# A list scheduler's numbers replaced in a one-core sparse attention and SwiGLU kernel

## The chip, the cores and the metric

The kernel runs on one core of a Trainium2 chip. The metric is the device time of one launch in microseconds, as the median of several runs. The chip has five engines that each follow their own instruction list in order: PE (matrix products), DVE (vector work), ACT (activation functions and copies), POOL (the third element-wise engine, here also the gathers) and SP (which here only starts transfers). They wait for one another through semaphores.

## The reference, cut to what matters

```python
# q, k, v: [4 batches, 8 heads, 768 rows, 64]; sampled_blocks: [24, 3]
scores = matmul(q, k.T) / sqrt(64)
mask = |row//32 - col//32| <= 1                     # window of 3 blocks
mask |= row block 0 or 23, or column block 0 or 23  # full rows and columns
mask |= column block in sampled_blocks[row block]   # 3 random blocks
attn = exp(scores - max) / (sum + 1e-9)             # over the masked entries
x = matmul(attn, v).transpose(0, 2, 1, 3).reshape(3072, 512)
g, val = x @ w_gate, x @ w_val                      # 512 -> 1536
out = (g * sigmoid(g) * val) @ w_out                # 1536 -> 512
```

All inputs are single precision values that reach the kernel as 64-bit words. The three weights are 512 x 1536, 512 x 1536 and 1536 x 512.

## The kernel before

The 3072 tokens are worked in eight chunks of 384 (half a batch each, three tiles of 128 tokens). A chunk is attention over its 12 query blocks of 32 rows with all 8 heads (11 sparse blocks and one full row block), and then the feed-forward part (FFN) on the 384 tokens. Names such as `b2.1.4` are chunk 2, tile 1, block 4.

Ahead of everything stand the inputs. Weights come in 36 pieces of 512 KB (L389) into a ring of four buffers (`w1raw`, `w2raw`), and three DVE operations turn each piece into single precision (`to_f32`, L382 to L384: one "decode"). Each piece is squared and summed on ACT (L361, `wsq`) and later split into a high and a low half-precision part (ACT L354, DVE L357). K and V of a batch come in three transfers each (L511), are squared and summed on ACT (L361), normalised to a power of two (PE L351, DVE L533 and L342 to L346) and split (L354, L357). K of batch 0 is then turned by PE (L583) and copied to `kst` by ACT and DVE (L593, L591); V goes back to memory (`vd`, L617) and is read again block by block (L1011 to L1013 on SP, and a gather on POOL, L1016) into `vring`. Queries come at L684 and L744, are split, and are spread out by L755 into `qs` (four transfers each).

One sparse block of attention is a chain: copy of its random K blocks into `kring` (L1002 to L1005; on POOL for chunk 0, else on DVE), scores on PE (L1051 and L1060 in chunks 0 and 1, L1030 after), maximum on DVE (L1069 or L1076), exponential on ACT (L1095), reciprocal on DVE, split of the probabilities (ACT L354, DVE L357), a transposing transfer that SP starts (L1155, `pts<-pp`), and the product with V on PE (L1168, `pv`). In chunk 0 PE transposes the probabilities instead (L1115, with copies at L1124 and L1128). The full row blocks run through L806, L817 to L835, L858 and L875. The FFN of chunk 0 works in single precision (`ffn_first`, L1255 and L1291), so that it needs decoded weights and not split ones; the FFN of the others uses half precision parts (`ffn`: first layer L1369 with 12 products for each of the 24 half-pieces, tanh L1373, products on DVE L1376 and L1379, split L1387 on ACT and L1390 on POOL, second layer L1416, out through L1305 and L1315).

The order is not written out by hand. Each piece of work is a task, given by `add(engine, microseconds, emit, needs, rank, ...)`. `Plan.order` runs a simulated clock over all tasks: an engine that is free takes, among the tasks whose needs have ended and whose buffers are free, the one of lowest rank. The rank is a base number plus an entry of the table `SHIFT` (L41 to L89) for the task's name. The order in which tasks are taken is the order in which their instructions are emitted, so that it fixes each engine's program; the numbers of microseconds are used for nothing else. `in_turn` keeps the blocks of one stage in the same order. A transfer is a task on SP with a duration `dma` of its own, which runs on one simulated queue and ends `DMA_US` later. The four lines that do this are

```python
t.rank = rank + SHIFT.get(t.key, 0.0)
if best is not None and (t.rank, t.no) > (best.rank, best.no): continue
queue = max(queue, t.end) + t.dma
t.end = queue + DMA_US
```

Of the kernel before, what the change touches and what calls it, by code (L numbers as in the profile page):

```python
# [11 lines left out]
I32 = mybir.dt.int32  # L12
# [8 lines left out]
DM, DF, DO = H * D, 1536, 512  # L21
# [11 lines left out]
K0, V0, TAB = -6.0, -3.0, -2.0  # L33
EVAC = -100.0
V_AT = 0.0
DMA_US = 2.0
SEM_US = 0.1
# [1473 lines left out]
```

## Time and profile before

| what | value |
|---|---|
| median of 3 runs | 847.31 us (847.08 to 849.96) |
| the profiled execution, its own time | 845.61 us |
| span of the profiled execution | 843.8 us |
| mean granted PE clock | 0.965 |
| PE busy | 769.2 us, 91% of the span |
| DVE, ACT, POOL busy | 592.1 us (70%), 528.4 us (63%), 200.7 us |
| bytes moved | 144.05 MB |

The profile is one execution. "Busy" is the time in which an engine executes; the wait of an instruction is the idle time just ahead of it, put down to what ended it. The granted clock is the share of PE's full speed that it had. The rest between the span and the run's own time (1.8 us) lies outside the recorded instructions.

### The profile page before, as it was taken

The page shows a single profiled execution, that of the slowest core. Times are in us where ns is not written, and L with a number is a line of the kernel's source. Part 1 is how long each engine was busy: PE and PEld are TensorE (multiplying, and loading weights), DVE is VectorE, ACT ScalarE, POOL GpSimd, SP SyncE. Part 2 cuts the span into 40 slices and gives each one's busy share as a digit, 9 for nine tenths or more (in the row PEclk, how much of TensorE's full clock was granted, in tenths as well). Part 3 has the DMA queues.
Part 4 walks back from the last instruction along what each step waited for, and adds up shares of the span by engine and source line. Part 5 has one row for each costly group of instructions (what it writes and reads, how often), then busy time and mean ns, then how long its engine had stood idle before and what let it go on. Part 6 is the DMA issues. An engine that isn't in the chain of part 4 may idle for free.

```text
span 843.8 us, 20625 instructions
## 1 busy us (share of the span) xinstructions
PE 769.2 (91%) x7634; PEld 460.9 (55%) x7634; DVE 592.1 (70%) x1784; ACT 528.4 (63%) x1266; POOL 200.7 (24%) x258
## 2 busy tenths in 40 slices
PE   0267799979999999999999999998999999999997
PEld 0246655545465655665566556663566556655653
DVE  5987989858888976896488757852679769821320
ACT  5855845669786766788467757873458658821220
POOL 5574100002014321231223211321123212310220
PEclk9757999989999999999999999999999999999999
DMA  9999785789947897899878876988847964820001
GB/s 292 256 280 274 213 241 164 146 200 185 220 128 220 186 228 138 191 180 232 218 179 180 182 167 132 199 173 243 210 96 143 193 145 103 169 57 26 1 1 38
DMA packets 196309, 144.05 MB, mean 171 GB/s; under 512 B 133104, under 2 KB 156272, under 8 KB 196208
## 3 DMA queue, kind: packets, MB, share of 16 engines
q1 hardware_dynamic: 190576, 125.42, 65.2%
q0 software_dynamic: 5632, 17.31, 8.3%
q8 instruction: 60, 0.98, 0.5%
q14 instruction: 41, 0.34, 0.1%
HBM read 86.58 MB, written 12.58 MB: 118 GB/s over the span
## 4 chain that ended last, share of the span: by engine, by line
PE 68%; DMA 15%; DVE 7%; ACT 3%; issue 3%; SPq 2%; POOL 1%; DVEq 0%; ACTq 0%; POOLq 0%
PE p L1369 33%; PE po L1416 13%; DMA pts<-pp 6%; PE pv L1168 6%; PE p L1255 5%; PE po L1291 4%; PE qk L1030 3%; DMA w<-vd 2%; DVE w L383 2%; DVE w L384 1%; PE pvf L875 1%; DMA qn<-in_q_dram 1%; DMA kraw<-in_k_dram 1%; PE qkf L806 1%; DMA qs<-qraw 1%
## 5 line engine op out<-in xcount | busy, mean ns | idle before, releaser
L1369 PE MATMUL p<-xt,w 128*128 128x384 f16 x2016 | 340.3, 326 | 0.0
L1369 PEld LDWEIGHTS <-w 128*128 128x128 f16 x2016 | 191.9, 98 | 128.4 <-issue 6.2
L1416 PE MATMUL po<-w,h 128*128 128x512 f16 x756 | 171.1, 381 | 0.0
L1390 POOL TENSOR_TENSOR h<-act,h 128x384 f16<-128x384 f32 x84 | 80.0, 953 | 304.4 <-ACT h L1387 304.1
L1016 POOL DMA_INDIRECT vring<-vd,vidx x82 | 78.6, 959 | 280.4 <-PE pv L1168 236.9
L1416 PEld LDWEIGHTS <-h 128*128 128x128 f16 x756 | 71.9, 98 | 87.2 <-issue 7.1
L1376 DVE SCALAR_TENSOR_TENSOR act<-act,p 128x384 f32<-128x384 f32 x84 | 46.1, 549 | 64.3 <-ACT act L1373 62.6
L1168 PEld LDWEIGHTS <-vring 128*128 128x128 f16 x1968 | 68.9, 99 | 28.2 <-issue 16.2
L357 DVE SCALAR_TENSOR_TENSOR pp<-e,rr,pp 128x256 f16<-128x256 f32 x152 | 77.7, 552 | 7.5 <-ACT pp L354 6.2
L1168 PE MATMUL pv<-pts,vring 128*128 128x64 f16 x1968 | 72.3, 194 | 11.0 <-DMA pts<-pp 6.3
L1373 ACT ACTIVATE act<-p,gsc 128x384 f32<-128x384 f32 x84 | 48.4, 577 | 52.8 <-PE p L1369 45.2
L1095 ACT ACTIVATE e<-e,nb,es 128x256 f32<-128x256 f32 x132 | 78.2, 593 | 2.2
L1387 ACT CAST h<-act 128x384 f16<-128x384 f32 x84 | 42.5, 505 | 54.4 <-DVE act L1379 53.9
L354 ACT ACTIVATE pp<-e,rr 128x256 f16<-128x256 f32 x152 | 67.8, 497 | 10.3 <-DMA ptsf<-ppf 3.6
L1255 PE MATMUL p<-xt,w 128*128 128x384 f32 x192 | 70.1, 520 | 1.3 <-ACT xt L1134 1.0
L1379 DVE SCALAR_TENSOR_TENSOR act<-act,hs,p 128x384 f32<-128x384 f32 x84 | 51.3, 611 | 22.9 <-PE p L1369 21.7
L1255 PEld LDWEIGHTS p<-xt,w 128*128 128x128 f32 x192 | 37.6, 202 | 27.6 <-issue 5.3
L1076 DVE CUSTOM_DVE_ANT_1 e<-qk,msk 128x256 f32<-128x256 f32 x132 | 50.0, 416 | 0.5 <-PE qk L1030 0.3
L1005 DVE COPY kring<-kst 128x256 f16 x228 | 46.0, 258 | 4.9 <-PE pv L1168 1.6
L1305 ACT ACTIVATE ot<-po,oc 128x512 f32<-128x512 f32 x21 | 14.4, 686 | 52.7 <-PE po L1416 52.2
L1194 DVE TENSOR_TENSOR xt<-pv,xt 64x256 f16<-64x256 f32 x76 | 31.9, 420 | 17.2 <-ACT xt L1189 14.1
L361 ACT ACTIVATE wsq<-w 128x512 bf16<-128x512 f32 x36 | 22.6, 628 | 25.6 <-DVE w L384 16.4
(168 smaller groups left out, 983.0 us busy)
## 6 DMA issues: line engine op xcount, KB each, us to landing
vring<-vd SPq DMA_DIRECT2D x82, 192.0 KB
w1raw<-in_w_dram SPq DMA_DIRECT2D x24, 512.0 KB
qs<-qraw SPq DMA_DIRECT2D x84, 128.0 KB
qn<-in_q_dram SPq DMA_DIRECT2D x48, 128.0 KB
w2raw<-in_w_dram SPq DMA_DIRECT2D x12, 512.0 KB
vfull<-vd SPq DMA_DIRECT2D x12, 512.0 KB
qraw<-in_q_dram SPq DMA_DIRECT2D x42, 128.0 KB
out_dram<-ot SPq DMA_DIRECT2D x20, 256.0 KB
```

Source lines behind the costliest of these rows:

```text
L354: nc.scalar.activation(hi, src, AF.Copy, scale=scale)
L357: nc.vector.scalar_tensor_tensor(lo, src, scale, hi, op0=ALU.mult, op1=ALU.subtract)
L1016: nc.gpsimd.indirect_dma_start(vf[0:96, 1, :], None, bt.vd, bass.IndirectOffsetOnAxis(ap=vidx[0:96, qb : qb + 1], axis=0))
L1076: nc.vector.tensor_tensor_reduce(ev[:, g], stv[:, g], o.g.msk[:, qb, :].unsqueeze(2).broadcast_to([P, 8, BLK]), scale=1.0, scalar=-3.0e38, ...
L1095: nc.scalar.activation(ev[:, g], sv[:, g], AF.Exp, bias=nb_[:, g : g + 1], scale=o.g.es[:, 0:1], accum_out=c["rs"][:, g : g + 1],)
L1168: nc.tensor.matmul(pvv[:, j, n % 2], vg[:, cc, l, 2 * j : 2 * j + 2, :], pq[:, g, m, cc, u : u + 2, :], start=i == 0, stop=i == 5,)
L1255: nc.tensor.matmul(buf.tile[:, 0:T], wst[m][:, f + 1, k_ * P : (k_ + 1) * P], x_f32()[:, k_, :], start=k_ == 0, stop=k_ == NKT - 1,)
L1369: nc.tensor.matmul(t[:, 0:T], w_[:, f, m, k_, :], xt.tile[:, l, k_, :], start=i == 0, stop=i == 11)
L1373: nc.scalar.activation(get(act, f"act_{ci}_{f}"), pg.tile[:, 0:T], AF.Tanh, scale=c["gsc"][:, f : f + 1])
L1379: nc.vector.scalar_tensor_tensor(act.tile, act.tile, c["hs"][:, 1:2], pw.tile[:, 0:T], op0=ALU.mult, op1=ALU.mult)
L1390: nc.gpsimd.tensor_tensor(hv()[:, 1, :], act.tile, hv()[:, 0, :], op=ALU.subtract)
L1416: nc.tensor.matmul(po.tile, hv[:, l, ts_], wo16[:, f, m, :], start=f == 0 and i == 0, stop=f == NF - 1 and i == 2)
```

## The change

It changes numbers alone, but for one need of one task. The same instructions stand in both programs (PE has 14,609 rows in both); their order differs.

1. All entries of `SHIFT` are replaced.
2. `DMA_US` goes from 2.0 to 2.2, `SEM_US` from 0.1 to 0.16, and a transfer may occupy the simulated queue from 0.4 us after SP began to start it, not only after SP has started all of it.
3. Nearly all durations are replaced. Those of SP grow most, by a factor of 5 to 22; POOL's grow; most of DVE, ACT and PE shrink a little.
4. The norm of the third weight (`norm` in `split_w2`, on PE) now also needs the last split of the first two weights; until now only the step after it did.

```diff
-DMA_US = 2.0
-SEM_US = 0.1
+DMA_US = 2.2
+SEM_US = 0.16
 SHIFT = {
-    "a0.0": -105.32, "a0.1": 0.02, "a0.2": -38.31, "a1.0": -72.7, "a1.1": -11.99, "a1.2": -2.34, "a2.0": -13.58, "a2.1":
...
-                    queue = max(queue, t.end) + t.dma
+                    queue = max(max(queue, now + min(0.4, t.us)) + t.dma, t.end)
                     t.end = queue + DMA_US
...
-    t_rep = add("POOL", 8.0, repeats, [t_tab], rank=TAB)
+    t_rep = add("POOL", 17.0, repeats, [t_tab], rank=TAB)
...
-        a = add("SP", 0.06, lambda: nc.sync.dma_start(get(raw, name).bitcast(I32), src.bitcast(I32)),
+        a = add("SP", 0.42, lambda: nc.sync.dma_start(get(raw, name).bitcast(I32), src.bitcast(I32)),
                 before, rank, take=[raw], dma=1.7)
-        return add("DVE", 1.85, lambda: to_f32(dst, raw.tile.bitcast(I32)), [a] + need, rank, use=[raw])
+        return add("DVE", 1.8, lambda: to_f32(dst, raw.tile.bitcast(I32)), [a] + need, rank, use=[raw])
...
-        t = add("PE", 0.15, norm, sq, rank + 0.2, take=[n])
-        t = add("DVE", 1.4, scale, [t, w1_split[-1][0]], EVAC, use=[n])
+        t = add("PE", 0.15, norm, sq + [w1_split[-1][0]], rank + 0.2, take=[n])
+        t = add("DVE", 1.3, scale, [t, w1_split[-1][0]], EVAC, use=[n])
...
-            t = add("SP", 0.12 * len(some), load, [], rank, take=hold[:1], dma=1.2 * len(some))
+            t = add("SP", 1.27 * len(some), load, [], rank, take=hold[:1], dma=1.2 * len(some))
...
-        o.done = add("SP", 0.24, spread, [t], rank, take=[qs], use=hold, dma=1.8)
+        o.done = add("SP", 2.4, spread, [t], rank, take=[qs], use=hold, dma=1.8)
...
-        vl = add("SP", 0.18 if vnew else 0.06, values, bt.v_done + vfree[vslot], rank + V_AT, dma=1.4 if vnew else 0.8)
+        vl = add("SP", 1.4 if vnew else 0.47, values, bt.v_done + vfree[vslot], rank + V_AT, dma=1.4 if vnew else 0.8)
...
-            kc = add("POOL" if first else "DVE", (2.0 if new else 1.2) if first else 1.0 if new else 0.55, keys,
+            kc = add("POOL" if first else "DVE", (3.4 if new else 1.25) if first else 0.75 if new else 0.42, keys,
...
-            a = in_turn("exp", "ACT", 1.8, power, [a], rank, use=[e])
+            a = in_turn("exp", "ACT", 1.45, power, [a], rank, use=[e])
...
-            a = add("SP", 0.06, turn, [a], rank, take=[pts], use=[pp], dma=1.8)
+            a = add("SP", 1.3, turn, [a], rank, take=[pts], use=[pp], dma=1.8)
```

Three places show what this does to the programs. The first is the head of SP's program, from the first weight piece on (`qn` are queries, `in_k_dram` and `in_v_dram` are K and V). Before:

```order
L389 DMA w1raw_1_122<-in_w_dram 128x1024
L684 DMA qn_126<-in_q_dram 64x4x128 x2
L684 DMA qn_129<-in_q_dram 64x4x128 x2
L684 DMA qn_132<-in_q_dram 64x4x128 x2
L389 DMA w1raw_1_135<-in_w_dram 128x1024
L389 DMA w1raw_0_137<-in_w_dram 128x1024
L389 DMA w1raw_0_139<-in_w_dram 128x1024
L511 DMA w_101<-in_k_dram 128x2x512 x3
L511 DMA w_99<-in_v_dram 128x2x512 x3
```

After:

```order
L389 DMA w1raw_1_122<-in_w_dram 128x1024
L389 DMA w1raw_1_126<-in_w_dram 128x1024
L684 DMA qn_139<-in_q_dram 64x4x128 x2
L684 DMA qn_142<-in_q_dram 64x4x128 x2
L684 DMA qn_145<-in_q_dram 64x4x128 x2
L511 DMA w_101<-in_k_dram 128x2x512 x3
L511 DMA w_99<-in_v_dram 128x2x512 x3
L389 DMA w1raw_0_233<-in_w_dram 128x1024
```

K has two weight pieces ahead of it instead of four. Further down, the spread of the third query tile (`qs_2`) stands ahead of the 27 reads of V (L1011 to L1013) instead of behind them, and the first of these reads is now that of block 1 (`vring_0`), which was fifth.

The second place is DVE between the query norm (`siq`) and the K norm (`kn`). Before:

```order
L346 TENSOR_SCALAR siq_334<-p_q_335 128x1
L382 TENSOR_SCALAR w_100<-w1raw_1_135 128x512
L383 SCALAR_TENSOR_TENSOR w_100<-w1raw_1_135,w_100 128x512
...
L384 SCALAR_TENSOR_TENSOR w_99<-w1raw_0_139,w_99 128x512
L357 SCALAR_TENSOR_TENSOR qsq_199<-qn_126,siq_334,qsq_199 128x512
L357 SCALAR_TENSOR_TENSOR qsq_326<-qn_129,siq_334,qsq_326 128x512
L357 SCALAR_TENSOR_TENSOR qsq_328<-qn_132,siq_334,qsq_328 128x512
L533 TENSOR_REDUCE kn_385<-nrm_k_381 128x1
```

After:

```order
L346 TENSOR_SCALAR siq_306<-p_q_307 128x1
L357 SCALAR_TENSOR_TENSOR qsq_227<-qn_139,siq_306,qsq_227 128x512
L357 SCALAR_TENSOR_TENSOR qsq_241<-qn_142,siq_306,qsq_241 128x512
L533 TENSOR_REDUCE kn_330<-nrm_k_328 128x1
```

Three decodes no longer stand there; one of them moved ahead of `siq`, so that two instead of four are ahead of `kn`. Counted on to the last transposed probabilities of chunk 0, 15 decodes stand ahead instead of 19. On ACT the squares of two weight pieces likewise no longer stand ahead of the third square of K. On POOL the three `kring` copies of chunk 0 stood in the order of blocks 2, 3, 1 and now stand in the order 1, 2, 3.

The third place is PE at the start of the FFN of chunk 1, where the attention of chunk 2 begins (`p_1_1` is the second piece of that FFN, `nrm_v1` and `nrm_k1` the norms of batch 1, `qk_1_1` the first scores of chunk 2). Before:

```order
L351 MATMUL nrm_v1_3543<-vacc_1_3464,ones_h_83 128x3
L1369 LDWEIGHTS w1_100
L1369 MATMUL p_1_1_3546<-xt_1_125,w1_100 128x384
...
L1369 MATMUL p_1_1_3546<-xt_1_125,w1_100 128x384
L1030 LDWEIGHTS qs_6_3488
L1030 MATMUL qk_1_1_3573<-kring_1_110,qs_6_3488 32x256
```

After:

```order
L351 MATMUL nrm_k1_3555<-kacc_1_3513,ones_h_83 128x3
L1369 LDWEIGHTS w1_100
L1369 MATMUL p_1_1_3558<-xt_1_125,w1_100 128x384
...
L1369 MATMUL p_1_6_3790<-xt_1_125,w1_100 128x384
L1030 LDWEIGHTS qs_6_3673
L1030 MATMUL qk_1_1_3818<-kring_1_110,qs_6_3673 32x256
```

The norm of K of batch 1 has moved behind that of V, and the first scores of chunk 2 now stand behind five more pieces of the FFN (`p_1_2` to `p_1_6`, 24 products each). The first product with V moved by one piece, from behind `p_1_8` to behind `p_1_9`.

## Rows read from the trace of the kernel before

**Rows 1.** Stretches: length, busy us (instructions) by engine, PE clock, DMA share, GB/s.

```profile
7.00:102.46 95.46, 47.06 (x842) 38.69 (x841) 80.83 (x193) 68.67 (x170) 50.55 (x94) 0.78 0.94 270
102.46:231.30 128.84, 122.53 (x968) 68.65 (x969) 108.49 (x293) 85.25 (x201) 7.21 (x8) 0.95 0.83 194
102.46:160.00 57.54, 57.32 (x241) 32.12 (x243) 52.11 (x118) 29.73 (x73) 0.33 (x1) 0.95 0.70 202
231.30:321.18 89.88, 87.76 (x901) 52.39 (x900) 72.45 (x226) 64.92 (x158) 26.02 (x27) 1.00 0.79 191
321.18:745.00 423.82, 417.27 (x4398) 250.93 (x4397) 311.75 (x1028) 289.75 (x706) 104.45 (x110) 1.00 0.82 173
```

**Rows 2.** Timeline of PE: start, duration, operation, idle before and releaser.

```profile
21.15 0.16 PE L351 MATMUL nrm_k<-kacc,ones_h 128*128 128x3 bf16 x1 [9.38 <-ACT w L361]
...
43.01 0.46 PE L1051 MATMUL qk<-kring,qs 128*32 128x160 f16 x8 [9.62 <-POOL kring L1005]
75.82 0.24 PE L1051 MATMUL qk<-kst,qs 128*32 128x96 f16 x1 [4.28 <-DMA qs<-qsq]
100.59 0.83 PE L1168 MATMUL pv<-pts,vring 128*128 128x64 f16 x23 [2.95 <-DVE pts L1128]
102.46 2.29 PE L1255 MATMUL p<-xt,w 128*128 128x384 f32 x3 [1.04 <-ACT xt L1134]
239.04 1.06 PE L1030 MATMUL qk<-kring,qs 128*32 128x256 f16 x32
240.03 9.92 PE L1369 MATMUL p<-xt,w 128*128 128x384 f16 x60
269.53 0.25 PE L1168 MATMUL pv<-pts,vring 128*128 128x64 f16 x3
```

**Rows 3.** DVE groups up to 102.46: count, busy us, mean ns, idle before.

```profile
L384 DVE SCALAR_TENSOR_TENSOR w<-w1raw,w 128x512 int32<-128x512 int32 x17 | 12.1, 714 | 0.6
L383 DVE SCALAR_TENSOR_TENSOR w<-w1raw,w 128x512 int32<-128x512 int32 x17 | 12.0, 708 | 0.6
...
L382 DVE TENSOR_SCALAR w<-w1raw 128x512 int32<-128x512 int32 x17 | 7.5, 440 | 4.2 <-DMA w1raw<-in_w_dram 4.2
...
L357 DVE SCALAR_TENSOR_TENSOR w<-w,ks 128x512 f16<-128x512 f32 x6 | 4.3, 757 | 0.4 <-ACT w L354 0.4
```

**Rows 4.** Timeline of SP, which starts transfers: start, duration, transfer, count.

```profile
23.26 8.64 SPq L755 DMA_DIRECT2D qs<-qsq  x8
49.93 0.36 SPq L1011 DMA_DIRECT2D w<-vd  x1
69.12 2.88 SPq L755 DMA_DIRECT2D qs<-qsq  x4
```

**Rows 5.** Timeline of POOL: the `kring` copies of the first three blocks.

```profile
33.28 0.46 POOL L1003 COPY kring<-kst 128x256 f16<-128x256 f16 x1 [6.39 <-DVE kst L591]
36.09 0.85 POOL L1002 COPY kring<-kst 128x256 f16<-128x256 f16 x1
```

**Rows 6.** Waits of PE from 102.46 to 745: total us, times, longest.

```profile
PE pv L1168 <- DMA pts<-pp: 6.3, 7, 2.6
PE qk L1051 <- ACT e L1095: 3.3, 1, 3.3
PE nrm_k L351 <- ACT k L361: 2.8, 1, 2.8
```

**Rows 7.** The chain that ended last, one transposing transfer: start, duration.

```profile
304.68 4.85 DMA pts<-pp
```

**Rows 8.** The page's groups on one block's chain: busy us, mean ns, idle before.

```profile
L357 DVE SCALAR_TENSOR_TENSOR pp<-e,rr,pp 128x256 f16<-128x256 f32 x152 | 77.7, 552 | 7.5 <-ACT pp L354 6.2
L1095 ACT ACTIVATE e<-e,nb,es 128x256 f32<-128x256 f32 x132 | 78.2, 593 | 2.2
L354 ACT ACTIVATE pp<-e,rr 128x256 f16<-128x256 f32 x152 | 67.8, 497 | 10.3 <-DMA ptsf<-ppf 3.6
L1076 DVE CUSTOM_DVE_ANT_1 e<-qk,msk 128x256 f32<-128x256 f32 x132 | 50.0, 416 | 0.5 <-PE qk L1030 0.3
```

More of the change, by code (lines that the diff above doesn't have):

```diff
@@ L411, in square_w @@
         sq = Buf("sq")
-        return add("ACT", 0.82, lambda: sumsq(wst[m][:, f + 1, :], acc, get(sq, f"wsq_{m}_{f}")[:, 0:DO]),
+        return add("ACT", 0.65, lambda: sumsq(wst[m][:, f + 1, :], acc, get(sq, f"wsq_{m}_{f}")[:, 0:DO]),
                    [w_f32[m][f]], rank, take=[sq])
@@ L418, in split_w @@
         before = w_read[m][f - 1] if f else []
-        t1 = add("ACT", 0.72, lambda: hi_part(hi, src, scale), need + before + [last], rank)
-        return add("DVE", 0.75, lambda: lo_part(lo, src, scale, hi), [t1], rank)
+        t1 = add("ACT", 0.63, lambda: hi_part(hi, src, scale), need + before + [last], rank)
+        return add("DVE", 0.67, lambda: lo_part(lo, src, scale, hi), [t1], rank)
     def split_w1(rank):
@@ L439, in scale @@
                 )
-            t = add("PE", 0.15, norm, sq + [x[0] for x in w1_split[-1:]], r, take=[n])
-            t = add("DVE", 0.8, scale, [t], EVAC, use=[n])
+            t = add("PE", 0.08, norm, sq + [x[0] for x in w1_split[-1:]], r, take=[n])
+            t = add("DVE", 0.75, scale, [t], EVAC, use=[n])
             for f in (f2, f2 + 1):
@@ L537, in load_kv @@
         t = add("PE", 0.12, norm, sq, rank, take=[n])
-        t = add("DVE", 0.9, scale, [t], EVAC, use=[n])
+        t = add("DVE", 0.7, scale, [t], EVAC, use=[n])
         if what == "k":
@@ L570, in load_kv @@
                 pi = parts[i : i + 1]
-                h_ = add("ACT", 0.72, high, [t] + los, rank, take=pi if first else [], use=ru + ([] if first else pi))
-                l_ = add("DVE", 0.75, low, [h_], rank, use=ru + pi)
+                h_ = add("ACT", 0.63, high, [t] + los, rank, take=pi if first else [], use=ru + ([] if first else pi))
+                l_ = add("DVE", 0.68, low, [h_], rank, use=ru + pi)
                 los.append(l_)
@@ L611, in load_kv @@
                     f0 = i == 0 and tt == 0
-                    done.append(add("SP", 0.06, turn, [l_], rank, behind=None if f0 else done[0], take=[bt.ks] if f0 else [],
+                    done.append(add("SP", 1.3, turn, [l_], rank, behind=None if f0 else done[0], take=[bt.ks] if f0 else [],
                                     use=pi + ([] if f0 else [bt.ks]), dma=1.7))
@@ L620, in put @@
                     )
-                done.append(add("SP", 0.06, put, los, rank, use=parts[i : i + 1], dma=1.6))
+                done.append(add("SP", 0.5, put, los, rank, use=parts[i : i + 1], dma=1.6))
             bt.last_lo = los[-1]
@@ L763, in load_q @@
         if not at:
-            need.append(add("SP", 0.12, load, [], rank, behind=g.loaded, take=hold, dma=1.2))
-        t = add("ACT", 0.72, lambda: hi_part(two()[:, 0, :], raw_q(), g.siq[:, 0:1]), need, rank, use=hold)
-        t = add("DVE", 0.75, lambda: lo_part(two()[:, 1, :], raw_q(), g.siq[:, 0:1], two()[:, 0, :]), [t], rank, use=hold)
-        o.done = add("SP", 0.24, spread, [t], rank, take=[qs], use=hold, dma=1.8)
+            need.append(add("SP", 1.27, load, [], rank, behind=g.loaded, take=hold, dma=1.2))
+        t = add("ACT", 0.63, lambda: hi_part(two()[:, 0, :], raw_q(), g.siq[:, 0:1]), need, rank, use=hold)
+        t = add("DVE", 0.67, lambda: lo_part(two()[:, 1, :], raw_q(), g.siq[:, 0:1], two()[:, 0, :]), [t], rank, use=hold)
+        o.done = add("SP", 2.4, spread, [t], rank, take=[qs], use=hold, dma=1.8)
         return o
@@ L836, in inv @@
                 recip(rs[:, 2:3], rs[:, 3:4])
-            s = in_turn("qk", "PE", 0.9, scores, [o.done] + bt.k_done, rank, take=qk, use=[o.qs, bt.ks])
-            m = [in_turn("top", "DVE", 0.55 + 0.35 * i, lambda i=i, f=top: f(i), [s, tsc], rank, use=[qk[i]]) for i in range(2)]
+            s = in_turn("qk", "PE", 0.87, scores, [o.done] + bt.k_done, rank, take=qk, use=[o.qs, bt.ks])
+            m = [in_turn("top", "DVE", 0.47 + 0.3 * i, lambda i=i, f=top: f(i), [s, tsc], rank, use=[qk[i]]) for i in range(2)]
             x = []
             for i in range(2):
-                x.append(in_turn("exp", "ACT", 0.85, lambda i=i, f=power: f(i), m, rank, take=[] if i else eb,
+                x.append(in_turn("exp", "ACT", 0.66, lambda i=i, f=power: f(i), m, rank, take=[] if i else eb,
                              use=[qk[i]] + (eb[1:] if i else [])))
             full_exp[0] = x[1]
-            r = add("DVE", 0.5, inv, x, rank)
+            r = add("DVE", 0.45, inv, x, rank)
             there, turned = [], []
@@ L860, in turn @@
                     )
-                a = in_turn("high", "ACT", 0.61, high, [r], rank, take=[pp], use=[eb[i]])
-                a = in_turn("low", "DVE", 0.62, low, [a], rank, use=[pp, eb[i]])
-                there.append(add("SP", 0.06, turn, [a], rank, take=[pts], use=[pp], dma=1.3))
+                a = in_turn("high", "ACT", 0.5, high, [r], rank, take=[pp], use=[eb[i]])
+                a = in_turn("low", "DVE", 0.54, low, [a], rank, use=[pp, eb[i]])
+                there.append(add("SP", 1.27, turn, [a], rank, take=[pts], use=[pp], dma=1.3))
             def product(j=j, turned=turned):
@@ L881, in product @@
                             )
[L883 removed]
+            pvs.append(in_turn("pv", "PE", 0.68, product, there + vl, rank, take=[] if j else [pv],
                                use=turned + vbuf + ([pv] if j else [])))
@@ L906, in low @@
             )
-        a = add("DVE", 0.7, gather, pvs, rank, take=[xs], use=[pv])
+        a = add("DVE", 0.6, gather, pvs, rank, take=[xs], use=[pv])
         a = add("ACT", 0.42, high, [a, x_open(ci, rank)], rank, use=[xs, xts[ci]])
@@ L1276, in ffn_first @@
                 if m == 0:
-                    a = add("ACT", 0.58, tanh, [last], EVAC, take=[act], use=[pg])
-            a = add("DVE", 0.56, mul_g, [a], EVAC, use=[act, pg])
+                    a = add("ACT", 0.38, tanh, [last], EVAC, take=[act], use=[pg])
+            a = add("DVE", 0.46, mul_g, [a], EVAC, use=[act, pg])
             hb = hbuf[f // 2]
-            h_done.append(add("DVE", 0.62, mul_w, [a, last], EVAC, take=[hb] if f % 2 == 0 else [],
+            h_done.append(add("DVE", 0.46, mul_w, [a, last], EVAC, take=[hb] if f % 2 == 0 else [],
                               use=[act, pw] + ([hb] if f % 2 else [])))
@@ L1316, in put @@
                 p0 = p1
-        a = add("ACT", 0.69, evac, [product, scaled], EVAC, take=[ot], use=[po])
-        add("SP", 0.1, put, [a], EVAC, use=[ot], dma=0.9)
+        a = add("ACT", 0.57, evac, [product, scaled], EVAC, take=[ot], use=[po])
+        add("SP", 0.6, put, [a], EVAC, use=[ot], dma=0.9)
     def ffn(ci, rank):
@@ L1350, in scale @@
             nc.vector.scalar_tensor_tensor(c["oc"], iv, iv, hs[:, 2:3], op0=ALU.mult, op1=ALU.mult)
-        a = add("ACT", 1.8, squares, x_done[ci], EVAC, take=[sq], use=[xt])
-        a = add("PE", 0.7, norms, [a], rank - 1000.0, take=[xn], use=[sq])
-        scaled = add("DVE", 1.6, scale, [a, w1_split[-1][0]], EVAC, use=[xn])
+        a = add("ACT", 1.4, squares, x_done[ci], EVAC, take=[sq], use=[xt])
+        a = add("PE", 0.66, norms, [a], rank - 1000.0, take=[xn], use=[sq])
+        scaled = add("DVE", 1.2, scale, [a, w1_split[-1][0]], EVAC, use=[xn])
         hbuf = [Buf("h") for _ in range(NF // 2)]
@@ L1394, in ffn @@
             w = last = add("PE", 1.95, lambda x=pw, m=mm: m(x, wv16), [g, parts[1]], r, take=[pw], use=[xt])
-            a = add("ACT", 0.58, tanh, [g, scaled, sc_t], EVAC, take=[act], use=[pg])
-            a = add("DVE", 0.56, mul_g, [a], EVAC, use=[act, pg])
-            a = add("DVE", 0.62, mul_w, [a, w], EVAC, use=[act, pw])
+            a = add("ACT", 0.48, tanh, [g, scaled, sc_t], EVAC, take=[act], use=[pg])
+            a = add("DVE", 0.47, mul_g, [a], EVAC, use=[act, pg])
+            a = add("DVE", 0.53, mul_w, [a, w], EVAC, use=[act, pw])
             hb = hbuf[f // 2]
-            a = add("ACT", 0.52, high, [a], EVAC, take=[hb] if f % 2 == 0 else [], use=[act] + ([hb] if f % 2 else []))
-            h_done.append(add("POOL", 0.95, low, [a], EVAC, use=[act, hb]))
+            a = add("ACT", 0.42, high, [a], EVAC, take=[hb] if f % 2 == 0 else [], use=[act] + ([hb] if f % 2 else []))
+            h_done.append(add("POOL", 0.97, low, [a], EVAC, use=[act, hb]))
         prev = last
```

59 lines of the change are left out of this document (29 added, 30 removed), and 95 rows, old and new, of the table SHIFT.

## The prediction

> **What bounds the kernel now.** I read the table of stretches first [rows 1]. From 102.46 us, where the FFN of chunk 0 begins [rows 2], PE is busy almost without a break: 122.5 of 128.8 us to the FFN of chunk 1, 87.8 of 89.9 to that of chunk 2, 417.3 of 423.8 from there to 745. PE's list of instructions is the same after the change, so of these 642.5 us no order can give back more than the idle part: 6.3 + 2.1 + 6.6 = 15.0 us. What lies after 745 has the same order of work and is left at nothing. Ahead of 102.46 it is otherwise: of the 95.5 us from 7 on PE is busy for 47.1 and idle for 48.4, the transfers run at a share of 0.94 and 270 GB/s, and DVE is busy for 80.8. The start is thus bounded by two things that lie close together, bytes and DVE, and by the order in which these reach PE. That is where a new order has most to give, and the timeline of PE [rows 2] shows where PE stood: 9.38 us for the K norm (ended 21.15), 9.62 us for `kring` (43.01), 4.28 us for `qs` (75.82), 2.95 us for transposed probabilities (100.59).
>
> **The change, part by part: the start.** The K norm follows the three squares of K on ACT, and ACT was busy with squares of weights in between. Two pieces fewer (1.05 MB) are sent ahead of K, which at 270 GB/s is 3.9 us, and ACT's weight squares no longer stand between. So the K norm comes at about 17.2 instead of 21.15, and DVE has its three decodes of that place (each 0.44 + 0.71 + 0.71 = 1.86 us [rows 3]) behind it. The copies to `kst` end some 3.6 us earlier. The second half of the first scores waited for POOL: it copied for blocks 2 and 3 first, 33.28 to 43.0, three blocks at about 3.2 us each [rows 5]. With block 1 first, the wait of 9.62 us is cut by two blocks' copies, 6.5 us, and by the earlier `kst`: the first block has its scores at about 33 instead of 43.5. What is late next is DVE, which turns each block over (maximum, reciprocal, copies), and then V: its reads began at 49.93 [rows 4], behind the writes of V. With the six splits of V at one go they can begin at about 46. The product of block 1 now stands on PE ahead of the scores of blocks 7 and on, so it is these reads that PE meets first. The spread of query tile 2 began at 69.12, behind the 27 reads of V [rows 4]; now it is ahead of them, and the wait at 75.82 (4.28 us, and 0.7 us a microsecond later) goes. It costs the V reads 4 x 0.7 = 2.9 us of SP, at a time when PE has scores to do.
>
> How much of this reaches 102.46 is bounded by the two resources. DVE: four decodes fewer are ahead of the end of chunk 0's attention, 7.4 us, and two splits of weights, 1.5 us (0.76 us each, by those of K, which have the same shape [rows 3]): 80.8 becomes 71.9. If its idle 14.6 us stay, the FFN starts 8.9 us earlier; if half of them go, 16. Bytes: four pieces fewer (2.1 MB) at 270 GB/s are 7.8 us. If neither counts but only the wait for `qs`, 4 us remain. I take 9.5 us, near the DVE bound with a little of its idle time gone: the FFN of chunk 0 starts at 93, with 88 and 98.5 as ends.
>
> At this place a rule of the notes speaks against the change. The Trainium skill, page "DMA: Bandwidth & Descriptors", section "Issuing engines are not separate DMA queues", says that the time a sequencer spends to start a transfer is usually small beside the transfer. The trace differs on the spreads of queries: eight of them occupy SP for 8.64 us [rows 4], and one transfer is started for each 128 KB, which at 270 GB/s takes 0.5 us. By the rule, new start times in the planner's table would be worth next to nothing, which is the second rival below with its 847; by the row they are worth a place in the order.
>
> **The FFN of chunk 0.** The four decodes come back here, and two splits: 8.9 us more for DVE. In 102.46 to 160 it was already busy for 52.1 of 57.5 us, 91% [rows 1], while PE hardly waited; to 231.3 it was busy for 108.5 of 128.8. PE's work there stays at 122.5 us, so with 117.4 us of DVE in about 126 the share is 93%. Before, PE lost 6.3 us there, 3.3 for an exponential and 2.6 at the most for one transposed block [rows 6], both in the second half of chunk 1's attention. In the new order that attention lies a little later against the FFN (its first product with V behind 75.0 us of PE work counted from the head of the list, was 71.9; its last behind 100.0, was 95.7, by the order and PE's mean durations), which gives the chain more room. So the decodes cost and the later place gives. I take 4 us of PE waits, with 2 and 8 as ends: a gain of 2.3 us (4.3 to -1.7). The FFN of chunk 1 starts at 93 + 126.5 = 219.5 instead of 231.3.
>
> **Chunk 2 and what follows.** Its first scores now stand behind five more pieces of the FFN (they began at 239.04 [rows 2]), 24 products of 0.165 us each (60 took 9.92 [rows 2]) or some 19.5 us of PE, and its first product with V (269.53) only one piece later. The room between the two falls from 29.8 to 14.2 us of PE work. One block's chain, with no queue, is two each of 0.42 us on DVE, 0.59 on ACT, 0.50 on ACT and 0.55 on DVE [rows 8], 4.1 us, with 0.5 us of scores, and a transfer of 4.85 us [rows 7]: 9.5 us. So 14.2 us leaves 4.7 for queueing. DVE's work from the FFN of chunk 1 to that of chunk 2 rises, since it starts earlier and ends at the same count: by the order with mean durations the sums at the two ends are 212.7 and 287.9 us, were 216.5 and 287.9, so 75.2 us for 87.8 us of PE, 86%. Waits of 2.1 us were there; I take 4 (1 to 8): a loss of 2 us.
>
> From 321 to 745 PE lost 6.6 us. The single wait of 2.8 us for a K norm [rows 6], that of batch 3, goes, since that norm now stands behind `p_4_3`, 1,470 rows of PE ahead of the first scores that use it, and stood 260 ahead. The other waits are mostly for transposed blocks. The new order leaves less room in places (the least in chunk 6 is 11.2 us of PE work, was 13.2; in the second halves of batches 1 to 3 some 13.6, were 15 to 19), 1.7 us above the chain of 9.5. I take 2.2 us of new waits there, 0 and 7 as ends: a gain of 0.6 us (2.9 to -4.1). The other durations (exponentials, tanh, POOL's copies) act through the same places only. The added need of the third weight's norm costs nothing by itself: that norm feeds splits that the second layer of chunk 1's FFN needs, 46 us of first-layer products after 231; if it came late, `po` of chunk 1 would wait.
>
> **The sum.** 845.61 (the profiled execution) - 9.5 - 2.3 + 2.0 - 0.6 = 835.2. The median of the runs is 1.7 us above that execution, so about 837. With all ends at once it is 845.6 - 14.5 - 4.3 - 1.1 - 2.9 + 1.7 = 824.5, and 845.6 - 4 + 1.7 + 5.9 + 4.1 + 1.7 = 855.
>
> **The rivals.** First, DVE takes back the start: decodes and splits moved behind 93 have to be done before the FFN of chunk 1 in any case, and if its queue does not get shorter than in 102 to 160 (91%), PE waits for as much as it gained there. For it speaks the sum of DVE up to the FFN of chunk 2, which is equal in both orders (287.9 us); against it, that it was busy for only 72.5 of the last 89.9 us. Then only some 4 us of the start last: 843 to 844.
>
> Second, the order does not matter: the start is a matter of bytes and of total DVE work (0.94 and 80.8 of 95.5 us [rows 1]), and the same bytes and decodes are needed by 231 us. Then nothing moves by more than 2 us: 846 to 848. The rule above would give this. Against it speak the single waits of rows 2, each of which has an order as its cause.
>
> Third, slower: chunk attention squeezed against its products with V. PE takes its list in order, so that a late `pts` block stops the FFN products behind it. The chain's room falls in at least five places to 11 to 14 us, and DVE has 0.86 and more there. If the queues add more than 4 us to the chain, PE waits for 2 to 3 us at each of the pairs of blocks that follow (some six pairs in chunks 2, 4 and 6): 15 to 18 us. It decides from the point where this passes the 11.8 us gained up to the FFN of chunk 1, and gives some 851. For it speaks that seven such waits were there with more room [rows 6]; against it, their size, 0.9 us in the mean.
>
> **How the numbers follow.** The forecast (start moved by 6 to 15 us, and most of it kept) has 0.66, and an own range of 826 to 841.5; the first rival 0.15, the second 0.10, the third 0.09. A measurement of this kernel tells about 0.5% from no change, 4.2 us: faster means below 843.1, slower above 851.5. The forecast counts as faster, the first rival half so and half as same, the second as same, the third half as same and half as slower; That is 0.735 faster, 0.22 same, 0.045 slower. The range takes the forecast from its low end and reaches through the first rival and half the second: 825 to 847.
>
> **What would show it.** In the new profile: the K norm at 16 to 18.5; the first scores of the `kring` half before 36; no wait for `qs` near 70; the first single precision product of the FFN at 88 to 98; the FFN of chunk 1 at 214 to 225. If PE waits over 8 us between these two, the first rival holds; if the FFN starts after 100, the second; if waits for `pts` and `vring` after 231 add up to over 15 us, the third. I would be wrong in the size above all through DVE's idle time in the start, which no row of before shows.

## The result and the profile after

The changed kernel takes 841.02 us (median of 18 runs, 835.37 to 847.25), the kernel before 849.28 in the same comparison (18 runs, 843.55 to 855.36). The ratio is 0.9906 with a 95% interval of 0.9877 to 0.9935: faster by about 8 us. The forecast was 837 against 847.31, a ratio of 0.988.

One thing has to be known to read the profiles. Single executions of either kernel spread over some 12 us, and a profile is one of them. That of the changed kernel took 845.16 us, near the upper end of its runs; that of before took 845.61, below its median. The two differ by 0.45 us where the medians differ by 8.3, so their spans don't show the gain. What can be compared is where each stretch began, and that needs more than one profile. A second profile of each kernel (runs `e1_again` and `b_again` below) stands beside the first wherever it matters.

The stretches of the changed kernel, cut at the same places as in [rows 1] (columns as there):

```profile
7.00:97.24 90.24, 49.45 (x842) 41.06 (x841) 75.93 (x182) 65.05 (x161) 47.13 (x94) 0.90 0.93 268
97.24:223.72 126.48, 120.67 (x967) 66.64 (x968) 112.51 (x282) 88.40 (x211) 10.27 (x11) 0.96 0.82 210
223.72:316.45 92.73, 88.49 (x903) 52.03 (x902) 74.60 (x253) 64.97 (x158) 24.26 (x24) 1.00 0.85 185
316.45:745.00 428.55, 417.54 (x4310) 248.99 (x4309) 302.88 (x1020) 287.96 (x700) 103.86 (x108) 1.00 0.80 167
```

The FFN of chunk 0 begins at 97.24 (was 102.46), that of chunk 1 at 223.72 (was 231.12, just ahead of the cut at 231.30 in [rows 1]), that of chunk 2 at 316.45 (was 321.18). Of the 7.4 us won by the FFN of chunk 1, this execution gives nearly all back behind it: up to 745 PE is idle for 15.3 us where it was idle for 8.7. PE's timeline has the same places as [rows 2]:

```profile
18.98 0.16 PE L351 MATMUL nrm_k<-kacc,ones_h 128*128 128x3 bf16 x1 [4.26 <-ACT w L361]
...
34.45 0.46 PE L1051 MATMUL qk<-kring,qs 128*32 128x160 f16 x8 [2.64 <-POOL kring L1005]
...
94.81 1.38 PE L1168 MATMUL pv<-pts,vring 128*128 128x64 f16 x23 [5.59 <-DVE pts L1128]
97.24 2.93 PE L1255 MATMUL p<-xt,w 128*128 128x384 f32 x4 [1.04 <-ACT xt L1134]
...
145.97 4.23 PE L1255 MATMUL p<-xt,w 128*128 128x384 f32 x8 [3.36 <-DVE w L384]
```

The last of these places in the kernel before:

```profile
137.80 4.14 PE L1255 MATMUL p<-xt,w 128*128 128x384 f32 x12 [0.22 <-DVE w L384]
```

The waits for ACT's squares, for `kring` and for `qs` have shrunk or gone. Two have grown: that for the last transposed copy from 2.95 to 5.59 us, and that for a weight decode in the middle of the FFN from 0.22 to 3.36 us. DVE's timeline says where the first comes from:

```profile
86.27 0.68 DVE L1128 TENSOR_TENSOR pts<-pt,pts 128x512 f16<-128x512 f32 x1
86.87 0.46 DVE L382 TENSOR_SCALAR w<-w1raw 128x512 int32<-128x512 int32 x1
...
93.47 0.69 DVE L384 SCALAR_TENSOR_TENSOR w<-w1raw,w 128x512 int32<-128x512 int32 x1
94.08 0.68 DVE L1128 TENSOR_TENSOR pts<-pt,pts 128x512 f16<-128x512 f32 x1
```

Between the last two copies of chunk 0 (L1128) stand four decodes, 86.87 to 94.08, 7.2 us. In their course PE runs out of all other work and is left with the product that needs the second copy. Behind the FFN of chunk 2 the waits for transposed blocks grew, before and after:

```profile
PE pv L1168 <- DMA pts<-pp: 3.2, 5, 1.1
```

```profile
PE pv L1168 <- DMA pts<-pp: 7.0, 6, 2.7
PE nrm_k L351 <- ACT k L361: 1.8, 2, 1.6
```

PE's granted clock is not what makes the gain. Its mean over a run was 0.959 to 0.991 before and 0.969 to 0.988 after. Among the runs at 0.978 or more the median is 849.7 us before (17 of the 60 runs beside the experiments) and 841.5 after (14 of 30 runs), the same 8 us.

### The profile page after: what moved, and what is told of

It reads as the page before. It is cut to its first block, busy times and chain, and to the rows that moved or that the text cites. A ratio compares the mean times of both kernels' runs of the same rounds, so it can differ in the third digit from the quotient of the medians.

```text
span 843.3 us, 20624 instructions
## 1 busy us (share of the span) xinstructions
PE 770.2 (91%) x7634; PEld 460.4 (55%) x7634; DVE 586.0 (69%) x1784; ACT 527.3 (63%) x1266; POOL 199.9 (24%) x258
## 4 chain that ended last, share of the span: by engine, by line
PE 60%; DVE 16%; DMA 12%; ACT 4%; issue 3%; SPq 3%; DVEq 1%; ACTq 0%
PE p L1369 30%; PE po L1416 13%; DMA pts<-pp 5%; PE pv L1168 4%; PE p L1255 4%; PE qk L1030 3%; DMA kraw<-in_k_dram 3%; DVE w L383 2%; DMA qs<-qraw 2%; DVE w L384 2%; DVE pp L357 2%; DVE w L357 2%; PE qkf L806 1%; DVE w L382 1%; PE pvf L875 1%
## 5 line engine op out<-in xcount | busy, mean ns | idle before, releaser
L1390 POOL TENSOR_TENSOR h<-act,h 128x384 f16<-128x384 f32 x84 | 82.5, 982 | 312.1 <-ACT h L1387 312.0
L357 DVE SCALAR_TENSOR_TENSOR pp<-e,rr,pp 128x256 f16<-128x256 f32 x152 | 74.2, 530 | 8.8 <-ACT pp L354 4.4
L1189 ACT CAST xt<-pv 64x256 f16<-64x256 f32 x76 | 27.6, 364 | 25.8 <-PE pv L1168 23.7
L1090 ACT ACTIVATE nb<-mx,es 128x2 f32<-128x2 f32 x88 | 25.5, 290 | 29.0 <-DVE mx L1076 20.8
L1005 DVE COPY kring<-kst 128x256 f16 x228 | 41.7, 240 | 0.7 <-PE qk L1030 0.7
```

What stands on the lines that cost most here:

```text
L357: nc.vector.scalar_tensor_tensor(lo, src, scale, hi, op0=ALU.mult, op1=ALU.subtract)
L1390: nc.gpsimd.tensor_tensor(hv()[:, 1, :], act.tile, hv()[:, 0, :], op=ALU.subtract)
```

## The experiments

All of them use the changed kernel's file with one more function in place of the last loop. It emits the tasks as near to a given list as needs and buffers allow; given the changed kernel's own list, it emits the changed kernel's program.

```diff
-    for t in plan.order():
+    for t in follow(plan):
         t.emit()
```

What differs is the list. Ratios are against the kernel before, run beside them on the same chip; times are medians.

| run | ratio, 95% interval | us | FFN of chunk 0, of chunk 1 begins (profile) |
|---|---|---|---|
| changed kernel, first | 0.9906 (0.9877 to 0.9935) | 841.0 | 97.24, 223.72 |
| e1_again | 0.9909 (0.9879 to 0.9939) | 841.5 | 94.24, 223.89 |
| b_again (kernel before) | (one run) | 848.3 | 104.46, 233.62 |
| e2_copy_first | 0.9930 (0.9902 to 0.9958) | 843.3 | 96.72, 224.26 |
| e7_keep_first | 0.9909 (0.9878 to 0.9941) | 842.2 | 89.69, 226.12 |
| e10_decodes_after | 0.9856 (0.9833 to 0.9879) | 837.4 | 90.60, 221.44 |
| e11_kring_old | 0.9953 (0.9929 to 0.9978) | 846.4 | 97.79, 223.05 |
| e8_seam_clean | 0.9908 (0.9882 to 0.9934) | 841.0 | 93.33, 220.63 |
| e9_late_new | 1.0028 (1.0001 to 1.0055) | 852.4 | 104.41, 232.00 |
| e3_start_new | 1.0232 (1.0189 to 1.0276) | 868.3 | 96.76, not read |
| e4_rest_new | 1.0240 (1.0193 to 1.0287) | 869.3 | 104.06, not read |
| e5_first_new | 1.0116 (1.0078 to 1.0155) | 858.4 | 94.44, 222.32 |
| e6_second_new | 1.0136 (1.0094 to 1.0177) | 859.4 | 105.89, 232.72 |

**Second profiles.** The two unchanged kernels once more.

> The changed kernel once more, for a second profile and times beside the runs below. If the four weight decodes that stand ahead of the last transposed copy of chunk 0 set the start of the FFN in every execution, PE again waits 5 to 6 us there and the FFN of chunk 0 starts at 96 to 98. If that wait belongs to the one profiled execution, it is under 2 us here. Time by both: about 841, 1% under the kernel before.

> The kernel before once more, for a second profile: single executions of it spread by some 10 us. If that spread comes from the start, where transfers are the bound, the first FFN product moves by as much as the span against 102.46 and 843.8; if it comes from single late transfers behind it, waits for pts, vring or qs differ.

PE's timeline in the second profile of the changed kernel, at the place of the 5.59 us wait, and in the FFN:

```profile
87.67 0.50 PE L806 MATMUL qkf<-kst,qs 128*64 128x384 f16 x1 [3.28 <-DMA qs<-qraw]
90.35 1.46 PE L806 MATMUL qkf<-kst,qs 128*64 128x384 f16 x7 [2.17 <-DMA qs<-qraw]
91.74 1.46 PE L1168 MATMUL pv<-pts,vring 128*128 128x64 f16 x24
94.24 1.01 PE L1255 MATMUL p<-xt,w 128*128 128x384 f32 x1 [1.04 <-ACT xt L1134]
...
142.44 2.29 PE L1255 MATMUL p<-xt,w 128*128 128x384 f32 x3 [4.04 <-DVE w L384]
```

Everything comes 3 to 4 us earlier than in the first profile, and PE stands 5.45 us at about the same place, now for the queries of the full rows. The four decodes ran on DVE from 83.10 to 90.26 meanwhile, so that the last copy was no earlier than that in any case. So the wait for decodes is not an accident of one execution, but it can hide behind a transfer. The FFN of chunk 0 starts 3 us earlier than in the first profile, and the FFN of chunk 1 starts at the same time. The stretches of this profile (columns as in [rows 1]) are

```profile
7.00:94.24 87.24, 45.84 (x841) 37.27 (x840) 75.17 (x183) 65.17 (x162) 47.80 (x94) 0.82 1.00 275
94.24:223.89 129.65, 122.27 (x966) 67.95 (x967) 112.24 (x281) 88.39 (x211) 10.27 (x11) 0.95 0.85 207
```

The second profile of before begins its FFN 2.0 us later than the first, its next FFN 2.5 us later, and its span is 2.7 us longer: between these two the difference lies in the start.

The two pairs also show what comes behind. From the FFN of chunk 1 to the last instruction the profiles of before take 612.7 and 612.9 us, those of the changed kernel 619.6 and 619.7.

**Does the wait for the four decodes cost time?** The last copy is put ahead of them, in the list of tasks:

```diff
-d1.6 decode, d1.5 decode, d0.6 decode, d0.3 decode, b0.2.3 copy (L1128)
+b0.2.3 copy (L1128), d1.6 decode, d1.5 decode, d0.6 decode, d0.3 decode
```

> The changed kernel, but the last transposed copy of chunk 0 (L1128, block 12) stands ahead of the four decodes instead of behind them; nothing else moves. Theory (the start bounds, PE is the bound after it): the wait of 5.6 us goes, the FFN of chunk 0 starts at 91 to 92, and most of it lasts: 836 to 838, some 4 us under the changed kernel. Rival (DVE has to do the decodes before PE can go on in any case): the FFN starts earlier, waits of the same size come back at its products (3.4 us for a decode near 146 grow to 8), and the time stays within 1 us of 841.

It took 843.3 us, no faster than the changed kernel. ACT's timeline, and PE's behind it:

```profile
95.11 0.63 ACT L361 ACTIVATE wsq<-w 128x512 bf16<-128x512 f32 x1 [1.07 <-DVE w L384]
95.64 0.19 ACT L361 ACTIVATION_READ_ACCUMULATOR wsq<-w 128x1 f32 x1
95.73 0.94 ACT L1134 ACTIVATE xt<-pv,vs 64x256 f32<-64x256 f32 x2
```

```profile
96.72 2.93 PE L1255 MATMUL p<-xt,w 128*128 128x384 f32 x4 [7.98 <-ACT xt L1134]
```

The copy was early, but ACT's next step on the path (`xt`, L1134) stands on ACT behind the squares of the same four pieces, and these wait for the decodes. The wait moved from DVE's list to ACT's. So this run doesn't yet tell theory and rival apart, and the next two take it further step by step.

```diff
-d1.6 decode, d1.5 decode, d0.6 decode, d0.3 decode, b0.2.3 copy, b0.2.3 product, b0.2.3 xt
+b0.2.3 copy, b0.2.3 product, b0.2.3 xt, d0.3 decode, d0.3 square, d1.6 decode, d1.5 decode, d0.6 decode
```

> The changed kernel with the four decodes ahead of the FFN of chunk 0 put behind the last transposed copy and behind ACT's copy of the last product (L1134), the one that the next norm needs first among them. In the run where only the DVE copy moved, PE waited 8 us for that ACT copy, which stood behind the squares of the four decoded pieces. Theory (the decodes are due in any case, DVE is the bound up to the FFN of chunk 1): the FFN of chunk 0 starts at 89 to 92 and the FFN of chunk 1 within 1 us of 223.7; time 840 to 843. Rival (PE is the bound from its first FFN product): the FFN of chunk 1 starts at 218 to 220, time 836 to 838.

The FFN began at 89.69, and yet that of chunk 1 at 226.12. PE:

```profile
89.69 1.56 PE L1255 MATMUL p<-xt,w 128*128 128x384 f32 x4 [1.04 <-ACT xt L1134]
98.41 0.17 PE L351 MATMUL nrm_w<-wacc,ones_h 128*128 128x4 bf16 x1 [7.17 <-ACT ef L828]
```

A third instruction held the path: a norm of weights on PE takes a buffer that the exponential of the first full row tile (`ef`, L828) has to free, and on ACT that exponential stood behind the four squares, too. The next list puts that tile's maximum and exponential, and the first tanh of the FFN, ahead of three of the decodes as well:

```diff
-d1.6 decode, d1.5 decode, d0.6 decode, d0.3 decode, b0.2.3 copy, b0.2.3 product, b0.2.3 xt, f1.0 maximum, f1.0 exponential, p0.0, tanh
+b0.2.3 copy, b0.2.3 product, b0.2.3 xt, f1.0 maximum, f1.0 exponential, p0.0, d0.3 decode, d0.3 square, norm s1.2, p0.0, tanh, d1.6 decode, d1.5 decode, d0.6 decode
```

> The changed kernel with three of the four decodes ahead of the FFN of chunk 0 put behind all that the first products of that FFN and the norm of the weights behind them wait for: the last transposed copy, ACT's copy of the last product, the maximum and exponential of the first full row tile, and the fourth decode. In the run before, PE waited 7.2 us for that exponential. Theory (DVE and its decodes bound the way to the FFN of chunk 1): the FFN of chunk 0 starts at 89 to 92 with no wait over 3 us up to 105, waits come back later, and the FFN of chunk 1 starts at 222 to 225; time 840 to 843. Rival (PE bounds): the FFN of chunk 1 starts at 218 to 220, time 835 to 838.

It took 837.4 us (5 runs), ratio 0.9856: about 4 us under the changed kernel, the two intervals just touching, and the best of all runs. PE's timeline and the stretches:

```profile
90.60 1.56 PE L1255 MATMUL p<-xt,w 128*128 128x384 f32 x4 [1.04 <-ACT xt L1134]
92.67 0.16 PE L351 MATMUL nrm_w<-wacc,ones_h 128*128 128x4 bf16 x1 [0.52 <-ACT wsq L361]
...
97.36 0.85 PE L806 MATMUL qkf<-kst,qs 128*64 128x384 f16 x4 [2.68 <-DVE p_w L342]
...
142.31 2.29 PE L1255 MATMUL p<-xt,w 128*128 128x384 f32 x3 [3.95 <-DVE w L384]
```

```profile
7.00:90.60 83.60, 45.05 (x842) 36.56 (x841) 69.57 (x173) 62.36 (x154) 48.03 (x94) 0.96 0.98 270
90.60:221.44 130.84, 121.31 (x967) 66.88 (x968) 118.36 (x292) 91.00 (x219) 10.25 (x11) 0.96 0.86 217
```

Neither side holds whole: the time is the rival's, and the FFN of chunk 1 begins between the two. Of the 3.6 to 6.6 us by which the FFN of chunk 0 starts earlier, 2.3 to 2.5 reach the FFN of chunk 1, a third to two thirds. New among PE's waits is the one of 2.68 us for a norm's result on DVE (`p_w`); the wait for a decode at 142.31 is no longer than in the changed kernel (3.36 and 4.04 us). DVE is busy for 118.4 of 130.8 us there, and which of its work takes the rest back was not tried.

The list moves more than three decodes: an exponential and the tanh on ACT go ahead with the copy, and on SP the loads of four pieces of the third weight now stand behind a query load and a read of V, since their buffers come free later. SP's change stands in `e7` too, which won nothing. The others were not tried one by one.

**Does the order of the three `kring` copies matter?** One part of the change is undone on POOL (on DVE one decode, `d1.1`, then stands ahead of the first block's maximum, as near to the list as it goes):

```diff
-kring copies of chunk 0 on POOL: block 1, block 2, block 3
+kring copies of chunk 0 on POOL: block 2, block 3, block 1
```

> The changed kernel with one part undone: POOL copies the K blocks of chunk 0 in the order of blocks 2, 3, 1 again instead of 1, 2, 3. Theory (the first scores hold up all that follows in the start): they come at 40 to 42 instead of 34.5, the FFN of chunk 0 starts 4 to 6 us later, and the time rises by 3 to 6. Rival (the start is bound by transfers and DVE, so PE's first scores are hidden): the first scores come late, the FFN starts within 1.5 us of the changed kernel's, the time stays within 1.5 us of 841.5.

PE's timeline:

```profile
41.09 0.46 PE L1051 MATMUL qk<-kring,qs 128*32 128x160 f16 x8 [9.82 <-POOL kring L1005]
...
95.36 1.39 PE L1168 MATMUL pv<-pts,vring 128*128 128x64 f16 x23 [4.11 <-DVE pts L1128]
97.79 1.01 PE L1255 MATMUL p<-xt,w 128*128 128x384 f32 x1 [1.04 <-ACT xt L1134]
```

The first scores come 6.6 us later, as the theory has it, and by the ratios the time rises by about 4 us (by the medians, which are of two chips, by 5), with an interval that overlaps that of the changed kernel by 0.0006. Its profile, though, shows what the rival says: the FFN of chunk 0 begins within 0.6 us of the changed kernel's first profile, and that of chunk 1 earlier by 0.7. This execution (846.59 us) is close to the run's median, and it is behind the FFN of chunk 1 that it takes long, 621.8 us, where its list is the changed kernel's. So the times say that this order carries part of the gain, about half by the ratios; the trace doesn't show how, and the mechanism stays open.

**Is the gain made in the start or behind it?** Six runs join one order's beginning to the other's rest. Where the seam lay decided whether they could be read. The first pair cuts at the first FFN product:

```diff
+e3: tasks of the changed order up to p0.0, then the order before;  e4: the other way round
```

> The order of the changed kernel up to the first product of the FFN of chunk 0, and the order of the kernel before for all the rest. Theory (what is won is won in the start): the FFN starts near 97, and 5 us or more of the gain stay, 842 to 845. Rival (the gain lies in the later part, with later attention and an earlier K norm): 848 to 850.

> The counterpart: the order of the kernel before up to the first product of the FFN of chunk 0, the order of the changed kernel for all the rest. Theory: the FFN starts near 102, and the time is 846 to 849. Rival: 842 to 844, and the waits of PE after 231 us add up to less than the 8.7 us of before.

They came out 2.3% and 2.4% slower than before. At that point 45 tasks are done in one order and not in the other, and buffers are handed out in another sequence, so that 180 and 100 of the tasks behind the seam stood elsewhere than in either order. In `e3` PE then waited 14.9 and 11.7 us at two places of the FFN of chunk 0. The next pair cuts where only nine tasks differ:

```diff
+e5: the changed order up to o1.2, then the order before;  e6: the other way round
```

> The order of the changed kernel up to the second layer of the FFN of chunk 1, third tile (some 310 us into the run, where the two orders have done the same tasks but for nine small ones), the order of the kernel before from there on. Theory (the gain is made ahead of this seam): 838 to 843. Rival (the gain lies behind it): 847 to 850. The earlier cut at the first FFN product ran through work in progress; here hardly any lies across it, so no extra waits at the seam.

> The counterpart with the same seam: the order of the kernel before up to it, that of the changed kernel behind it. Theory: 848 to 854, no better than before, since the changed order shows 10.9 us of PE waits behind 330 us where that of before shows 6.6. Rival: 841 to 844.

They are 1.2% and 1.4% slower than before: nine tasks were enough to move 332 and 112 of the tasks behind the seam by way of the buffers. Up to the seam `e5` was as fast as the changed kernel (94.44, 222.32), and it lost behind it. These four tell nothing on the question; they show that orders cut and joined where buffers are in flight give a third order, and that this alone can cost 1 to 2%. The last pair uses seams that move 11 tasks and none:

```diff
+e8: the changed order up to o1.0, then the order before;  e9: the order before up to o3.0, then the changed one
```

> The changed order up to the second layer of the FFN of chunk 1 (first tile, some 270 us), the order of before from there on. The seam before this one moved some 330 tasks behind it by way of buffers that had been handed out in another sequence, which made its times useless; this seam moves 11. Theory (the gain is made in the first 230 us): 839 to 843. Rival (it is made behind): 847 to 850.

> The order of before up to the second layer of the FFN of chunk 3 (some 400 us), the changed order from there on, with a seam that moves no task. Theory (the changed order wins nothing behind 400 us, with the K norm of batch 3 out of the way and tighter chunks in its place): 848 to 852. Rival (its later part wins 3 us or more): 843 to 846.

`e8` has the ratio of the changed kernel with all of its order (0.9908 against 0.9906, each to within 0.0026 to 0.0029, some 2 us). So the gain is made ahead of 270 us, and by the times the two orders behind it are worth the same to within some 3 us. Its profile is its lowest execution (831.0 us of span):

```profile
93.33:220.63 127.30, 119.76 (x967) 66.68 (x968) 112.43 (x282) 88.39 (x211) 10.38 (x11) 0.97 0.84 210
220.63:745.00 524.37, 516.75 (x5380) 309.21 (x5379) 385.73 (x1285) 357.05 (x866) 129.46 (x135) 1.00 0.80 173
```

`e9` took 852.4 us, 0.28% over before with an interval that just clears 1: the late part of the changed order wins nothing and may cost 2 us. Its profile has one long wait on PE, at a place where neither unchanged kernel has one:

```profile
473.97 1.44 PE L1168 MATMUL pv<-pts,vring 128*128 128x64 f16 x24 [5.99 <-DMA pts<-pp]
```

The profiles speak for a larger loss. From the FFN of chunk 1 to the end `e8`, with the order of before behind its seam, takes 610.4 us, like the two profiles of before (612.7 and 612.9), and `e9` 616.3. The six profiles with the changed order take 612.5 (`e10`) to 621.8 (`e11`), 618 in the mean. How much the changed order loses there in the median, between nothing and some 6 us, the runs leave open.

## Why the prediction was right, and where its steps were off

**The bound.** Right: the gain is made ahead of 270 us (`e8`), and PE's busy time from the FFN of chunk 0 to 745 is the same in both to within 1 us (627.6 and 626.7).

**The start.** Forecast 9.5 us, measured 5.2 between the first profiles (102.46 and 97.24) and 10.2 between the second (104.46 and 94.24), 7.7 in the mean. Both ends lie within the range of 4 to 14.5, and that the mean comes near is in part luck, since two of its terms were off, in the same direction. The K norm came at 18.98 (19.25 in the second profile), outside the 16 to 18.5 that I gave, and not at 17.2: I counted the weight pieces ahead of K and not the one more that is sent ahead of the queries. The queries landed later for it: ACT's first instruction waits for them, its idle time is 10.05 us here and was 7.71, and from there to the last square of K ACT works without a break. ACT's timeline, of after and then of before:

```profile
10.05 1.28 ACT L361 ACT_TABLE_LOAD   x1 [10.05 <-DMA qn<-in_q_dram]
```

```profile
7.71 1.28 ACT L361 ACT_TABLE_LOAD   x1 [7.71 <-DMA qn<-in_q_dram]
```

The other is the bound by DVE, which gave 8.9 us less work ahead of the FFN of chunk 0. DVE was busy there for 75.93 us, not for 71.9: 4.9 us less than before, and 6.2 less in the second pair (75.17 against 81.35). Four decodes did leave the place ahead of the last copy, but the two splits of weights still stand ahead of the FFN's first product, behind the last copy; the first full-row maximum came in (1.2 us); and in the first profile one step of a decode took 2.23 us. DVE's idle time fell by 0.3 and by 4.0 us, which makes up the 5.2 and 10.2. Nor does a count show the place: four of the 15 decodes stand in one row directly ahead of the last copy. The terms for `kring` and `qs` held on PE: the first scores came at 34.45 (forecast: before 36), and no wait for `qs` stands near 70. But `e11` takes the first of them away, and its FFN of chunk 0 begins only 0.6 us later than in the one profile and 3.6 later than in the other, so that what the shorter wait is worth there stays open.

**The FFN of chunk 0.** Forecast 4 us of PE waits, measured 5.8 (126.48 less 120.67) and 7.4 in the second profile (129.65 less 122.27): no gain over the 6.3 of before instead of 2.3. DVE was busy for 112.5 us, fewer than the 117.4 of the sum, since less had left the start, but a decode still came late at 142 to 146. The waits stay under the 8 us from which the first rival, DVE taking the start back, was to hold; but it is part of the truth: in `e7` and `e10` the start of this FFN moved to 90, and the next FFN came 2 us later (`e7`) or 2.3 to 2.5 us earlier (`e10`). The FFN of chunk 1 began at 223.72 and 223.89, inside the forecast of 214 to 225; the gain there was 7.4 and 9.7 us and not 11.8.

**Chunk 2.** Forecast a loss of 2 us, measured 2.7 (92.73 against 90.06, counted from the first product). The waits, 4.2 us, are of another kind than forecast: 0.6 and 1.3 us for a maximum and 1.9 for `xt`, all on DVE, 0.5 for a K norm, and none for `pts`; that DVE's work of the FFN is what they queue behind was not tried.

**The rest.** Forecast a gain of 0.6, measured by the times nothing (`e8`) to a loss of 2 us (`e9`), and by the profiles a loss: from the FFN of chunk 2 to 745 PE is idle for 11.0 us and was for 6.6. The K norm of batch 3 no longer waits for 2.85 us, as forecast, but that of batch 2 now does, for 1.59 and 2.35 in the two profiles, since it moved too; I had looked at one norm only. The third rival, tighter chunks that cost PE, shows in the waits for `pts` (7.0 against 3.2 us in one execution), at a third of the size that would have turned the sign.

**The second rival**, that the order doesn't matter, falls: the same instructions in another order cost 2.3% in `e3`, `e11` loses some 4 us by the order of a few tasks, and `e10` wins some 4. Starting the eight spreads of queries again took SP 8.71 us, 1.1 us for each 128 KB. The rule of the Trainium skill that stood beside this rival (page "DMA: Bandwidth & Descriptors", section "Issuing engines are not separate DMA queues") says that starting a transfer usually takes little time beside the transfer itself. The trace doesn't agree for these spreads: by estimate 128 KB take 0.5 us at the 270 GB/s of the start. What the new start times alone are worth no run shows, since all numbers changed together.

The sum: 10.3 us forecast, 8.3 found in the medians. Up to the FFN of chunk 1 it was 11.8 forecast and 8.6 found (the mean of the two pairs of profiles); behind it a loss of 1.4 forecast and, by what is left of the median, one of 0.3, while the two pairs of profiles themselves lose 6.9 and 6.8 us there. The mechanism was right in the main, the start too large by 3 us. The measured ratio of 0.9906 lies between the forecast's 0.988 and the first rival's 0.995 (843 against 847.31), nearer to the forecast; the waits above speak against that rival too, though not by much (5.8 and 7.4 against its 8).

## What to carry to other kernels

Where engines follow their lists in order, look for the row that stands ahead of the critical step on each engine, not only for how much work does: four decodes ahead of one copy left PE waiting for 5.6 us, and moving the copy alone only showed the next engine on which the same four stood in the way. A faster start is worth only what the next bound lets through, so read the place where the two meet (here the FFN of chunk 1) before counting it. And when single executions spread wider than the effect, compare medians, and use more than one profile to see which waits recur and in which stretch the spread lies.

## What was unexpected of the hardware

POOL's copies ran at two speeds, and DVE's timeline beside them says when. POOL, and then DVE, in the changed kernel:

```profile
31.95 2.45 POOL L1005 COPY kring<-kst 128x256 f16 x3
...
37.55 0.85 POOL L1005 COPY kring<-kst 128x256 f16 x1
38.35 0.40 POOL L1002 COPY kring<-kst 128x256 f16<-128x256 f16 x1
```

```profile
33.27 4.88 DVE L357 SCALAR_TENSOR_TENSOR w<-w,vs,w 128x512 f16<-128x512 f32 x6
38.06 0.68 DVE L1069 TENSOR_REDUCE mx<-qk 128x2 f32<-128x512 f32 x1
```

While DVE splits V, a copy takes 0.85 us; beside the reduction that follows, 0.40. The three copies that the first scores waited for (from 31.95 on) took 0.82 us each, beside the end of a decode and the first splits of V, about twice the price of the undisturbed one. In the first profile of the changed kernel it also went the other way once. DVE, and then POOL:

```profile
66.20 2.23 DVE L382 TENSOR_SCALAR w<-w1raw 128x512 int32<-128x512 int32 x1
```

```profile
66.05 2.10 POOL L1005 COPY kring<-kst 128x256 f16 x6
```

This step of a decode takes 0.43 us at the median and ended just behind POOL's six copies (68.43 and 68.15); in the second profile none took over 0.65 us. That may be part of the 3 us between the starts of the two profiles. The Trainium skill, page "SBUF — State Buffer", section "SBUF: two separate sides", says that the two engines share a pair of ports that is locked for whole instructions, among others by a DVE instruction with two inputs in SBUF, as the splits are; the rows of POOL agree with that.

The other surprise was the spread: 12 us between single executions of one program on one core. In the second group of runs of the changed kernel the granted clocks, 0.969 to 0.988, don't order with the times (845.6 us of span at 0.980, 837.3 at 0.976).
